# FNet plus PEER layer on one core: adds for the rows of y on GpSimd, an earlier tie for the key scale, half of each token group normalized by VectorE, and the third chunk's weights split eight blocks sooner

## The chip, the cores and the metric

One core of a Trainium2 chip runs the whole kernel. The time is device microseconds of one execution, the median of several. A core has TensorE (PE, matrix products; its weight loads are listed as PEld), VectorE (DVE), ScalarE (ACT), GpSimd (POOL) and SyncE (SP, which issues most of the DMAs here). Each engine works through its own queue in order and waits on semaphores for what others make.

## The reference, cut to what matters

`x` has 2048 tokens of 512 numbers. The result is a sum of three parts, the last two from the layernormed tokens `xn`:

```
xn  = layernorm(x)
# FNet: real part of a DFT over the hidden dimension, then over the sequence
a, b = xn @ dft_hid_re.T, xn @ dft_hid_im.T
y    = dft_seq_re @ a - dft_seq_im @ b
# PEER: 32 heads; two sets of 64 keys of 128 numbers; 4096 experts
q      = xn @ w_q                                # 32 heads x (128 + 128)
s1, s2 = q1 @ k1.T, q2 @ k2.T                    # 64 scores each
take the best 2 of s1 and of s2, of the 4 sums the best 2, g = softmax of these
out    = sum over heads and both: g * gelu(xn . u[expert]) * v[expert]
return x + y + out
```

## The kernel before, in words

The Python text lists instructions; a scheduler of the framework then fixes the order in which each engine gets them, from their dependencies, their place in the text and its own estimate of times. So a text that comes later can still stand earlier in a queue, and several lines of the kernel exist only to tie an instruction to another (a copy with scale 0, a one-element copy into a buffer) so that it is not placed too soon.

**Tokens.** The 2048 tokens are 16 tiles of 128, in four groups of four (`g`, with tiles `q` 0 to 3). Groups are worked in the order `G = (1, 0, 2, 3)`; `n` is a group's place in that order. `ln(g, n)` (L331) makes mean and variance of four tiles, on VectorE (L356 `bn_stats`, L357 the aggregate into `mvs`) or, for two tiles of the second group and one of the fourth, on ScalarE (L342, L343). Then ScalarE takes a square root for the whole group (L360), and VectorE works out `rstd` (L364) and `negm` (L365). `ln_norm(g, n)` (L370) normalizes the four tiles in place, on VectorE (`norm`, L308) or on ScalarE (L379). Group 0, the second in order, uses for its tiles 2 and 3 a masked pair `nm0` in place of `negm` and `rstd`.

**First part of FNet.** `fold` (L402, its first instruction is L409, its last are L412 and L413) adds and subtracts mirrored tokens and columns on VectorE and leaves `Q`; `main` (L433, products at L442) multiplies `Q` with parts of the sequence matrix on TensorE, once per group for the real and once for the imaginary part. `sides` and `evict` finish this, with results in buffers that later hold `u`.

**Scores.** Instead of making `q`, the kernel multiplies `w_q` with the keys first: M = w_q·k, per chunk of four heads, eight chunks (`NCH`). `m_load` (L130) loads a chunk's `w_q` in four parts; `m_mul` (L135) multiplies with the keys (in f32 at L147 for the first two chunks, split in f16 parts at L143 for the others); `m_parts` (L218) writes M as a f16 high part (ScalarE, L221) and a f16 low part (VectorE, L222), four pieces each. The scales come from `w_scale` (L211), seven small VectorE instructions (L589, L118, L119, L121, L214, L215, L216), of which L589 is the tie:

```
nc.vector.tensor_scalar(wsc[:, 0:1], rstd[:, G[1], 0:1], 0.0, 1e-13, op0=ALU.mult, op1=ALU.add)
w_scale(wtot, wsc[:, 0:1])
```

It multiplies a number by 0 and adds 1e-13, the lower limit of the scale, so its only effect is when it can run. For the third and later chunks `m_prep(j, t, ...)` (L150) splits part `t` of the weights of chunk `j` (counted from 0): a f16 copy on ScalarE (L157), a scaled f32 copy on GpSimd for two of the parts (L161) and on ScalarE for the other two (L159), and the subtraction on GpSimd (L162). `s_mm` (L243, products at L247) makes the scores of one token tile for one chunk in 12 products, in the order of the four pieces of M. Eight tiles of the first chunk are done ahead, by `early` (L273), while FNet's first part still runs; `stage` (L509) gives each tile its split form (L514, L515) and its transpose by DMA (L516).

**The loop over chunks and tiles** (from L941) runs over `j` and `i`; block `j * 16 + i` is one token tile of one chunk. `scores` (L878) has ScalarE evict the product (L889) and VectorE find the best (L893, L897). Around it the text hangs other work on block numbers: `HID` names the blocks at which `y_rows` (L687) makes one block of rows of `y`, and ten blocks later `y_store` (L698) writes it with three DMAs on SP; `todo` holds the splits of weights, the filling of `u` and `v` (L772 to L774) and more; `MST` names the tiles after which `m_stage` lets TensorE multiply the next chunk's weights; and the weights of chunk `j + 2` are loaded at tile 9 of chunk `j`. `routing` (L807) turns the best scores of a finished chunk into expert numbers and gates, partly on GpSimd (L822 to L862), with an exponential on ScalarE (L830).

**Rows of y.** `y_rows` calls `hid` (L519): four f32 products on TensorE into one PSUM bank (L521 to L524), seven ScalarE instructions that take the bank apart (L528 to L530), and four adds that combine even and odd columns in place (L533, L534). The bank comes from the two small pools (`pb`, `pc`, two banks each) that `m_mul` uses too.

**After the chunks** come the experts: products with `u` (L1025), gates written out as one-hot products (L1053 to L1063), products with `v` (L1108), the final sums, and tests of the symmetry of the DFT matrices hung in between. The change does not touch them.

Of the kernel before, what the change touches and what calls it, by code (L numbers as in the profile page):

```python
# [15 lines left out]
ALU = mybir.AluOpType  # L16
# [6 lines left out]
NT = S // P  # L23
H = 32
NCH = 8
# [9 lines left out]
def tile_fnet_peer(ctx, tc, x, ca, cb, c5, wt, wf, wr, wq, kt, ut, vn, out):  # L35
# [9 lines left out]
    nc = tc.nc  # L45
# [28 lines left out]
    mvs = cst.tile([P, 4, 4, 2], F32, name="mvs")  # L74
    rstd = cst.tile([P, 4, 4], F32, name="rstd")
# [16 lines left out]
    wsc = cst.tile([P, 4], F32, name="wsc")  # L92
# [87 lines left out]
    def m_fit(j, junk):  # L180
        nc.scalar.activation(junk, M[j][0][:, 0], AF.Abs, accum_out=fits[:, NW + 32 + j:NW + 33 + j])
# [29 lines left out]
    def w_scale(total, low):  # L211

        p, q = pow2(None, MP[0], "pw", 2, total, low)
        nc.vector.tensor_scalar(wsc[:, 0:2], q, 2.0 ** 19, None, op0=ALU.mult)  # L214
        nc.vector.scalar_tensor_tensor(sm0, q[:, 0:1], 2.0 ** 27, q[:, 1:2], op0=ALU.mult, op1=ALU.mult)  # L215
        nc.vector.scalar_tensor_tensor(inv1, p[:, 0:1], 2.0 ** -29 / XS, p[:, 1:2], op0=ALU.mult, op1=ALU.mult)  # L216
# [23 lines left out]
    def xn(g, q):  # L240
        return xp[2 * g + q // 2][:, q % 2]
# [49 lines left out]
    G = (1, 0, 2, 3)  # L291
# [15 lines left out]
    def norm(dst, src, i):  # L307
        nc.vector.tensor_scalar(dst, src, mvs[:, i // 4, i % 4, 0:1], rstd[:, i // 4, i % 4:i % 4 + 1],  # L308
                                op0=ALU.subtract, op1=ALU.mult)
# [60 lines left out]
    def ln_norm(g, n):  # L370
        for q in (0, 2, 1, 3):
            t = xn(g, q)
            b, r = negm[:, g, q:q + 1], rstd[:, g, q:q + 1]
            if g == 0 and q > 1:
                b, r = nm0[:, 0, q - 2:q - 1], nm0[:, 1, q - 2:q - 1]
            if n in (0, 3) and q % 2 == 0:
                norm(t, t, 4 * g + q)
            else:
                nc.scalar.activation(t, t, AF.Identity, bias=b, scale=r)  # L379
# [139 lines left out]
    def hid(t, ims, n, pre, pn, pim, bank):  # L519

        nc.tensor.matmul(bank[:n, 0:129], pre[0], wfs[:, 0:129], start=True, stop=True)  # L521
        nc.tensor.matmul(bank[:n, 129:257], pre[1], wfs[:, 129:257], start=True, stop=True)
        nc.tensor.matmul(bank[:n, 257:384], pim[0], wfs[:, 257:384], start=True, stop=True)
        nc.tensor.matmul(bank[:n, 384:512], pim[1], wfs[:, 384:512], start=True, stop=True)  # L524
        for d, v, a in ((t[:, 2:256:4], bank[:n, 0:127:2], 0), (t[:, 4:256:4], bank[:n, 1:127:2], 1),
                        (t[:, 256:258], bank[:n, 127:129], 1), (t[:, 513:514], bank[:n, 127:128], 1),
                        (t[:, 0:1], bank[:n, 128:129], 1)):
            nc.scalar.activation(d, v, AF.Identity, bias=pn[:, a:a + 1])  # L528
        nc.scalar.activation(t[:, 1:256:2], bank[:n, 129:257], AF.Copy)
        nc.scalar.activation(ims, bank[:n, 257:512], AF.Copy)  # L530
        for a, b, im in ((2, 259, ims[:, 0:127]), (1, 258, ims[:, 127:255])):
            e = slice(a, 256, 2)
            nc.vector.tensor_tensor(t[:, b:513:2], t[:, e], im, op=ALU.add)  # L533
            nc.vector.tensor_tensor(t[:, e], t[:, e], im, op=ALU.subtract)  # L534

    def load_x(g):
        for h in range(2):
# [48 lines left out]
    load_x(G[3])  # L586
    load(0, G[3], behind_stage)
    ln(G[1], 1)
    nc.vector.tensor_scalar(wsc[:, 0:1], rstd[:, G[1], 0:1], 0.0, 1e-13, op0=ALU.mult, op1=ALU.add)  # L589
    w_scale(wtot, wsc[:, 0:1])  # L590
    main(0, G[0])
    for kd in range(KD):
# [10 lines left out]
    for i in TO[4:6]:  # L603
        stage(i)
    ln(G[2], 2)
    ln_norm(G[2], 2)
    for b in range(4, 6):
        early(b)
# [105 lines left out]
    def part_b(safe, stS, stP, stE, xt, u_sb, cmp_p, w4):  # L714
# [10 lines left out]
        def behind(src, at):  # L725

            if at is None:
                return src
            nc.scalar.activation(at, src, AF.Copy)
            return at  # L730
# [4 lines left out]
        def am_load(which, g):  # L735
            nc.sync.dma_start(uf[15].rearrange("p (c f) -> p c f", c=2),
                              uvs[which][2 * g:2 * g + 2].rearrange("c p f -> p c f"))

        def absmax(which, g, at):
            nc.scalar.activation(uf[15], uf[15], AF.Abs, scale=behind(one, at), accum_out=asums[:, g, which:which + 1])  # L740
# [160 lines left out]

        MST = {1: 1, 3: 2, 5: 3, 6: 4, 8: 5, 10: 6} if safe else {3: 1, 4: 2, 5: 3, 7: 4, 8: 5, 9: 6}
        MST0 = MST if safe else {}
        HID = {13: 8, 14: 0, 15: 1, 16: 2, 17: 3, 30: 4, 31: 5, 32: 6, 33: 7}
        todo = [[] for _ in range(NCH * NT)]
        if safe:
            for which in range(2):
                for g in range(16):
                    am_load(which, g)
                    absmax(which, g, None)  # L910
            uv_scale()
            for t in range(7):
                m_stage(0, wq_tile, t)
        else:
            am_load(0, 0)
            for which, n in ((0, 10), (1, 15)):
                todo[n].append(lambda at, w=which: absmax(w, 0, at))
            todo[10].append(lambda at: am_load(1, 0))
            todo[18].append(lambda at: uv_scale())
            todo[20].append(lambda at: m_fit(0, uf[15].bitcast(F16).rearrange("p (k n) -> p k n", k=KD)))  # L920
            todo[(NCH - 1) * NT + 6].append(
                lambda at: m_fit(NCH - 1, MP[0].tile([P, 2, KD, 512], F16, tag="m", name="mj")[:, 0]))
            for j in range(2, NCH):
                for t in range(4):
                    todo[(j - 1) * NT + 2 * t - 4].append(
                        lambda at, j=j, t=t: m_prep(j, t, wqp, behind(sw, at)))
        fills = [(0, g) for g in (0, 1, 2, 3, 8, 9, 10, 11, 12, 13, 14, 4, 5, 6, 7, 15)] + [(1, g) for g in range(V2)]
        slots = [29, 31, 36, 43, 45] + [16 * j + i for j in range(3, 7) for i in (4, 6, 11, 13)]
# [12 lines left out]
        for j in range(NCH):  # L941
            if j + 1 == NCH:
                wq_st.close()
            if j == 0 and not safe:
                vals, idx = EV, EX
            else:
                vals = sp.tile([P, NT, 2, 8, HC], F32, tag="vals", name=f"vals{j}", bufs=2)
                idx = sp.tile([P, NT, 2, 8 if safe else 2, HC], U16, tag="idx", name=f"idx{j}", bufs=2)
            if j == 0 and not safe:
                for a, b in ((0, NT),):  # L950
                    nc.vector.tensor_copy(EV[:, a:b, :, 0, :], M[1][0][:, 1, 3, 8 * a:8 * b].rearrange(
                        "p (i w h) -> p i w h", w=2, h=HC))
            for i in range(NT):
                spare = scores(j, i, vals, idx)
                for t, f in ((j * NT + i, y_rows), (j * NT + i - 10, y_store)):
                    if t in HID and not safe:
                        f(HID[t])
                if j == 1 and not safe:
                    nc.sync.dma_start(xt_d[i], xt[i].rearrange("p a k n -> p (a k n)"))
                mst = MST if j else MST0  # L960
                if j + 1 < NCH and i in mst:
                    m_stage(j + 1, wq_tile, mst[i])
                if j == 0 and i == 6 and not safe:
                    alloc_v(0, V2)
                if j == 0 and 9 <= i < 13 and not safe:
                    sums(i - 9)
                if j + 2 < NCH and i == 9:
                    m_stage(j + 2, wq_tile, 0)
                if i in (1, 2, 4) and pend is not None:
                    routing((0, 2, None, 1)[i - 1], *pend)  # L970
                if j + 1 == NCH and i in (4, 7, 8):
                    routing((4, 7, 8).index(i), j, vals, idx, 0, 4, nc.vector)
                if j + 1 == NCH and i == NT - 1:
                    for b in range(2):
                        compact(b, z[:, b].rearrange("p w k t h -> p (w k t h)"), cmp_p, f"cmp{b}")
                    nc.sync.dma_start(z_d[2:4].rearrange("i p f -> p i f"),
                                      z[:, 2:4].rearrange("p i a k t h -> p i (a k t h)"))
                for n, f in enumerate(todo[j * NT + i]):
                    f(spare[:, n:n + 1])
            pend = (j, vals, idx)  # L980
# [374 lines left out]
        for ph in phases[2:]:  # L1355
            if ph[0] == "z":
                n = 4 * len(ph[1:]) - 2
# [21 lines left out]
        for n, ph in enumerate(phases):  # L1379
            if ph[0] == "z":  # L1380
                b = ph[1:]
# [7 lines left out]
            b = ph[1]  # L1389
# [44 lines left out]
    with tc.If(rv > 0):  # L1434
        with tc.tile_pool(name="gen", bufs=1) as gp, \
# [16 lines left out]
            for i in range(NT):  # L1452
                t = gload(x[i % 4, i // 4], [P, D], "x", f"gx{i}")
                norm(t, t, i)
                gx.append(gsplit(t, [P, D], "xs", f"gxs{i}", 1.0 / XS, NT))
            for q in range(4):
                ya = gp.tile([P, 4, D], F32, tag="ya", name=f"gya{q}")
                for ri in range(2):
                    pp = [gps.tile([P, 512], F32, tag="gp", name=f"gp{q}{ri}{d}", bufs=4)
                          for d in range(KD)]  # L1460
                    for i in range(NT):
                        t = gp.tile([P, 512], F32, tag="c", name=f"gc{q}{ri}{i}", bufs=2)
                        g, sq = divmod(i, 4)
# [14 lines left out]
                    for kd, pieces in enumerate((((0, 1, P, 0), (P - 1, 0, 1, 2)), ((0, 1, P, 1), (P - 1, 0, 1, 0)),  # L1478
                                                 ((0, 0, 1, 1), (1, 1, P, 2)), ((0, 0, P, 3),))):
                        t = gp.tile([P, 512], F32, tag="c", name=f"gw{q}{ri}{kd}", bufs=2)  # L1480
# [3 lines left out]
                    for a in range(4):  # L1484
                        py = pb(f"gy{q}{ri}{a}")
                        n = 0
# [9 lines left out]
                        b = 4 * a + q  # L1496
# [55 lines left out]
```

## Time and profile before

| | |
|---|---|
| time, median of 3 runs | 1153.36 us (1151.84 to 1153.71) |
| the profiled execution's own time | 1150.41 us |
| its span, first to last instruction | 1148.5 us |
| mean granted TensorE clock | 0.996 of full speed |
| busy: TensorE, weight loads, VectorE, ScalarE, GpSimd | 1132.9, 724.5, 945.2, 602.9, 229.0 us |
| scores and FNet | up to 420 us into the span |
| experts | from 420 us to the end |
| DMA, mean over the span | 146 GB/s |

The span's stages are read from the chain of work that ended last, in which TensorE's first product with `u` (L1025) stands at 420.54 us. Busy times overlap; a busy engine can still have nothing to do with the end. The busy time of TensorE counts matmuls whose ends are modelled, so its holes are a better guide than its share.

### The profile page before, as it was taken

What the parts mean: (1) busy time and instruction counts of PE and PEld (TensorE: products, weight loads), DVE (VectorE), ACT (ScalarE), POOL (GpSimd) and SP (SyncE); (2) the same over time, 40 slices, a digit from 0 to 9 for tenths busy, and PEclk for the clock granted to TensorE, in tenths of its full rate; (3) what the DMA queues carried; (4) which work ended last, traced back from release to release, by engine and by line L of the source; (5) the groups of instructions that cost most, each with busy time, mean ns of one, the idle gap of its engine ahead of it and who ended that gap; (6) DMA issues with size and microseconds to landing.
All of it is one profiled execution on the core that took longest, in us unless ns stands there. A gap on an engine that the chain in (4) does not pass through costs nothing.

```text
span 1148.5 us, 25267 instructions
## 1 busy us (share of the span) xinstructions
PE 1132.9 (99%) x9884; PEld 724.5 (63%) x9884; DVE 945.2 (82%) x2851; ACT 602.9 (52%) x1051; POOL 229.0 (20%) x229
## 2 busy tenths in 40 slices
PE   7999999999999999999999999999999999999997
PEld 5465554544545469687488478479569569558763
DVE  7899999899899999956985895896896796888570
ACT  6556687687687644353445445435536436433440
POOL 1303366675774400000000000000010010000000
PEclk8999999999999999999999999999999999999999
DMA  9973345234232105352742742743644555452423
GB/s 293 298 167 153 123 154 202 93 111 163 68 138 72 59 15 142 106 178 79 247 149 88 260 149 93 235 164 105 213 161 147 178 166 169 157 175 66 130 75 104
DMA packets 98334, 167.81 MB, mean 146 GB/s; under 512 B 32916, under 2 KB 48155, under 8 KB 98206
## 3 DMA queue, kind: packets, MB, share of 16 engines
q1 hardware_dynamic: 97904, 166.04, 44.6%
q8 instruction: 79, 1.29, 0.5%
q14 instruction: 49, 0.40, 0.1%
q10 hardware_dynamic: 302, 0.08, 0.0%
HBM read 142.69 MB, written 17.63 MB: 140 GB/s over the span
## 4 chain that ended last, share of the span: by engine, by line
PE 88%; DVE 8%; DMA 2%; ACT 1%; POOL 0%; issue 0%; SPq 0%; POOLq 0%; ACTq 0%
PE z L1025 29%; PE v L1108 28%; PE s L247 23%; PE g L1063 4%; PE p L442 2%; DVE vals L893 1%; PE m L143 1%; DVE idx L897 1%; DVE u L533 1%; DVE u L893 1%; DMA xt_d<-xq 1%; DVE u L897 1%; PE m L147 1%; DMA uv<-in_vn_dram 1%; DVE L L1053 0%; DVE u L534 0%
## 5 line engine op out<-in xcount | busy, mean ns | idle before, releaser
L1025 PE MATMUL z<-xb,u 128*128 128x256 f16 (+1 forms) x3840 | 342.7, 251 | 0.2 <-ACT w L1032 0.2
L1025 PEld LDWEIGHTS <-u 128*128 128x128 f16 x3840 | 309.7, 98 | 26.6 <-issue 0.3
L247 PE MATMUL s<-m,xq 128*128 128x512 f16 x1344 | 298.6, 380 | 4.5 <-DVE m L222 4.5
L1108 PE MATMUL v<-v,act 128*128 128x512 f16 x1056 | 233.2, 379 | 0.0
L247 PEld LDWEIGHTS <-xq 128*128 128x128 f16 x1344 | 130.1, 98 | 156.7 <-issue 7.7
L1053 DVE TENSOR_TENSOR L<-io_lam,cmp 128x2048 f16<-128x2048 f16 x128 | 156.0, 1219 | 59.4 <-PE g L1063 59.4
L1108 PEld LDWEIGHTS <-act 128*128 128x128 f16 x1056 | 101.4, 98 | 117.6
L1121 POOL TENSOR_TENSOR y<-y,xr 128x512 f32<-128x512 f32 x15 | 27.0, 1803 | 610.6 <-DMA y<-y_d 492.0
L1032 ACT ACTIVATE act<-z,scl 128x256 f32<-128x256 f32 (+1 forms) x152 | 72.4, 502 | 120.2 <-PE z L1025 120.2
L893 DVE MAX8 vals<-ss 128x8 f32<-128x64 f32 x896 | 133.9, 216 | 0.0
L1108 PE MATMUL v<-v,w 128*128 128x512 f16 x480 | 106.2, 379 | 0.0
L1184 ACT ACTIVATE cx<-cx 128x896 f32<-128x896 f32 x64 | 60.5, 945 | 70.2 <-DVE cx L1164 49.2
L889 ACT ACTIVATE ss<-s,wsc 128x512 f32<-128x512 f32 x120 | 79.7, 682 | 31.7 <-PE s L247 18.3
L897 DVE FIND_INDEX8 idx<-vals,ss 128x8 uint16<-128x256 f32 x224 | 93.9, 419 | 0.0
L1078 ACT ACTIVATE act<-w 128x1024 f16<-128x1024 f32 x36 | 48.3, 1358 | 60.5 <-DVE w L1071 60.1
L1108 PEld LDWEIGHTS <-w 128*128 128x128 f16 x480 | 46.1, 98 | 53.4
L1071 DVE SCALAR_TENSOR_TENSOR w<-act,scl,g 128x1024 f32<-128x1024 f32 x44 | 55.6, 1274 | 19.8 <-ACT act L1032 19.8
L1158 DVE TENSOR_TENSOR cx<-cx 128x512 f32<-128x512 f32 (+2 forms) x84 | 48.4, 609 | 24.4 <-DMA cx<-in_cb_dram 23.1
L1063 PEld LDWEIGHTS <-L 128*128 128x128 f16 x2048 | 60.6, 96 | 11.2 <-DVE R L1061 1.3
L1079 DVE TENSOR_TENSOR act<-w,act 128x1024 f16<-128x1024 f32 x44 | 60.3, 1372 | 3.7 <-ACT act L1078 3.7
L1061 DVE TENSOR_TENSOR R<-R,cmp 128x512 f16<-128x512 f16 x128 | 61.5, 481 | 1.5
L1063 PE MATMUL g<-R,L 128*128 128x32 f16 x2048 | 61.7, 176 | 0.3 <-DVE R L1061 0.2
(317 smaller groups left out, 1316.6 us busy)
## 6 DMA issues: line engine op xcount, KB each, us to landing
v<-v_d SPq DMA_DIRECT2D x67, 512.0 KB
cx<-in_cb_dram SPq DMA_DIRECT2D x64, 448.0 KB
w<-in_wq_dram SPq DMA_DIRECT2D x28, 512.0 KB
fit<-in_wq_dram SPq DMA_DIRECT2D x28, 512.0 KB
uv<-in_vn_dram SPq DMA_DIRECT2D x16, 512.0 KB
uv<-in_ut_dram SPq DMA_DIRECT2D x16, 512.0 KB
c<-in_ca_dram SPq DMA_DIRECT2D x8, 512.0 KB
y<-y_d SPq DMA_DIRECT2D x16, 256.0 KB
```

What stands on the lines that cost most here:

```text
L247: nc.tensor.matmul(ps, xt[i][:, l, kd, :], m[:, r, kd, :], start=(n == 0), stop=(n == 3 * KD - 1))
L889: nc.scalar.activation(s, ps, AF.Copy, scale=inv)
L893: nc.vector.max(vals[:, i, w, :, h], s[:, g, :])
L897: nc.vector.max_index(idx[:, i, w].rearrange("p k h -> p (k h)"), vals[:, i, w, 0:2].rearrange("p k h -> p (k h)"), s[:, w * HC:g + 1, :]. ...
L1025: nc.tensor.matmul(ps if n == 1 else ps.rearrange("p (b n) -> p b n", b=2), ug[:, l, c % 2, kd, :], xb2[:, k0, r, kd, :] if n == 1 else xb ...
L1032: nc.scalar.activation(ACT[bb][:, cg * m:cg * m + m, :], pv[:, i], AF.Gelu_apprx_tanh, scale=zsc)
L1053: nc.vector.tensor_tensor(L.rearrange("p t (l two) -> p t l two", two=2), io_lam.rearrange("p (l two) -> p l two", two=2).unsqueeze(1).to_ ...
L1061: nc.vector.tensor_tensor(Rv, Rv, bc(2, NC), op=ALU.mult)
L1063: nc.tensor.matmul(p[:, hf, t * NC:(t + 1) * NC], L[:, t, :], R[:, t, :], start=True, stop=True)
L1079: nc.vector.tensor_tensor(w16[..., 1], w, w16[..., 0], op=ALU.subtract)
L1108: nc.tensor.matmul(pv, w16[:, c, :, l], v_sb[g][:, r, cc, :], start=(n + cc == 0 and k == 0), stop=(n == 15 and cc == 1 and k == 2))
L1184: later.append(lambda: nc.scalar.activation(tf[:, P:], tf[:, P:], AF.Abs, accum_out=chk[:, n:n + 1]))
```

## The change

Five places, all before the experts:

- The four adds of each block of rows of `y` in `hid` go from VectorE to GpSimd.
- The tie of the key scale reads the mean of the second group's tile 3 (`mvs`) in place of that group's `rstd`.
- `ln_norm` normalizes tiles 0 and 2 on VectorE in every group; before, only in the first and the fourth. Tile 2 of group 0 takes its masked pair on VectorE in the form multiply, then add.
- Blocks 4 to 7 of the rows of `y` come at blocks 29 to 32, before at 30 to 33.
- The third chunk's weights (`j` = 2) are split at blocks 4, 6, 8 and 10, before at 12, 14, 16 and 18; and their loads are listed at tile 0 of the first chunk, before at tile 9. Other chunks keep their places.

```
@@ ln_norm
-            if n in (0, 3) and q % 2 == 0:
+            if q % 2 == 0 and g == 0 and q > 1:
+                nc.vector.tensor_scalar(t, t, r, b, op0=ALU.mult, op1=ALU.add)
+            elif q % 2 == 0:
                 norm(t, t, 4 * g + q)
             else:
                 nc.scalar.activation(t, t, AF.Identity, bias=b, scale=r)
@@ hid
-            nc.vector.tensor_tensor(t[:, b:513:2], t[:, e], im, op=ALU.add)
-            nc.vector.tensor_tensor(t[:, e], t[:, e], im, op=ALU.subtract)
+            nc.gpsimd.tensor_tensor(t[:, b:513:2], t[:, e], im, op=ALU.add)
+            nc.gpsimd.tensor_tensor(t[:, e], t[:, e], im, op=ALU.subtract)
@@ tie of the key scale
-    nc.vector.tensor_scalar(wsc[:, 0:1], rstd[:, G[1], 0:1], 0.0, 1e-13, op0=ALU.mult, op1=ALU.add)
+    nc.vector.tensor_scalar(wsc[:, 0:1], mvs[:, G[1], 3, 0:1], 0.0, 1e-13, op0=ALU.mult, op1=ALU.add)
@@ part_b
-        HID = {13: 8, 14: 0, 15: 1, 16: 2, 17: 3, 30: 4, 31: 5, 32: 6, 33: 7}
+        HID = {13: 8, 14: 0, 15: 1, 16: 2, 17: 3, 29: 4, 30: 5, 31: 6, 32: 7}
@@
-                    todo[(j - 1) * NT + 2 * t - 4].append(
+                    todo[(j - 1) * NT + 2 * t - (12 if j == 2 else 4)].append(
                         lambda at, j=j, t=t: m_prep(j, t, wqp, behind(sw, at)))
@@
-                if j + 2 < NCH and i == 9:
+                if j + 2 < NCH and i == (9 if j or safe else 0):
                     m_stage(j + 2, wq_tile, 0)
```

(`safe` marks a second copy of this code, with other scales, which is not entered for these inputs.)

## The prediction

> **What bounds the kernel now.** I read the page first, then busy time by stretches, then the order of instructions in the stretches where TensorE stood still. Span and TensorE's busy time come from the page:
>
> ```profile
> span 1148.5 us, 25267 instructions
> PE 1132.9 (99%) x9884; PEld 724.5 (63%) x9884; DVE 945.2 (82%) x2851; ACT 602.9 (52%) x1051; POOL 229.0 (20%) x229
> ```
>
> TensorE is idle for 1148.5 - 1132.9 = 15.6 us. The table by stretches says where (start:end, length, then busy time of PE, PEld, DVE, ACT, POOL, and the granted clock):
>
> ```profile
> 21.34:22.40 1.06, 0.01 (x1) 0.00 (x0) 1.06 (x5) 1.06 (x3) 0.00 (x0) 1.00 1.01 190
> 22.40:25.86 3.46, 0.00 (x1) 0.00 (x0) 2.74 (x10) 3.46 (x7) 0.00 (x0) 0.50 0.95 205
> 25.86:29.20 3.34, 3.34 (x8) 1.13 (x8) 3.34 (x8) 2.12 (x6) 0.00 (x0) 0.50 1.00 397
> ...
> 25.86:80.07 54.21, 54.21 (x220) 28.01 (x220) 48.43 (x107) 30.63 (x60) 11.06 (x19) 0.97 0.84 238
> 80.07:168.62 88.55, 86.89 (x552) 47.59 (x552) 86.62 (x460) 60.33 (x142) 38.75 (x38) 1.00 0.46 152
> 168.62:1130.00 961.38, 960.90 (x8936) 628.76 (x8936) 791.02 (x2227) 495.07 (x818) 175.23 (x152) 1.00 0.42 138
> ```
>
> One hole of 4.5 us ends at 25.86, one of 88.55 - 86.89 = 1.66 us ends at 168.62, and half a microsecond is spread over the next 961 us; the rest lies ahead of the first hole and after the last matmuls, where the change touches nothing. VectorE is busy 86.62 of 88.55 us in the stretch to 168.62, but TensorE hardly notices, so relief for VectorE is worth only what it takes out of the two holes. Their rows in order of time (start, length, engine, line, in brackets the idle time before and its releaser):
>
> ```profile
> 25.86 12.16 PE L247 MATMUL s<-m,xq 128*128 128x512 f16 x48 [4.51 <-DVE m L222]
> ...
> 168.62 0.22 PE L143 MATMUL m<-sums,wh 128*128 128x64 f16 x2 [1.66 <-ACT u L530]
> ```
>
> The first hole has a second price. The granted clock falls to 0.50 about 1.06 us after TensorE falls idle and stays there to 29.20: 8 matmuls take 3.34 us. The other 40 of the 48 take 12.16 - 3.34 = 8.8 us, 0.22 each, so the eight lose 3.34 - 8 x 0.22 = 1.6 us. The most that the change can give at these places is 4.5 + 1.6 + 1.66 = 7.8 us. By the Trainium skill ("TensorE: Matmul & The Clock Gate", Part 1: The HAM clock gate) the clock halves only after an idle window of about 3.4 us; here it fell sooner, so a shortened hole could still cost the 1.6 us, and a rival below counts that.
>
> **The key scale.** The first hole is the wait for the first chunk's M = w_q·k, which ScalarE (L221) and VectorE (L222) write as two halves once the scale is known:
>
> ```profile
> 16.52 0.17 DVE L357 BATCH_NORM_AGGREGATE mvs<-sums 128x2 f32<-128x6 f32 x1
> ...
> 17.67 3.68 PE L147 MATMUL m<-k_sb,wq 128*128 128x64 f32 x32
> ...
> 20.96 0.81 ACT L379 ACTIVATE x<-x,negm,rstd 128x512 f32<-128x512 f32 x1 [1.97 <-DVE negm L365]
> ...
> 21.10 0.14 DVE L589 TENSOR_SCALAR wsc<-rstd 128x1 f32<-128x1 f32 x1
> ...
> 22.95 0.16 DVE L215 SCALAR_TENSOR_TENSOR wsc<-pw 128x1 f32<-128x1 f32 x1
> ...
> 23.79 2.39 ACT L221 ACTIVATE m<-m,wsc 128x512 f16<-128x512 f32 x4
> ...
> 25.06 2.72 DVE L222 SCALAR_TENSOR_TENSOR m<-m,wsc,m 128x512 f16<-128x512 f32 x4
> ```
>
> The scale's small steps run from L589 at 21.10 to L215, done at 23.11: 2.0 us, with other work between. L589 reads rstd, the end of the group's statistics; after the change it reads the fourth tile's mean, which the aggregate at 16.52 writes by 16.69. So the scale can be known at 16.7 + 2.0 = 18.7. Then L221 (2.39 / 4 = 0.6 each) goes into ScalarE's 1.97 idle microseconds from 18.99 on. TensorE finishes w_q·k piece after piece, 3.68 / 4 = 0.9 apart, the last at 21.35; the first three copies can be done by 21.0, the fourth at 22.0, or at 22.8 behind one normalize. VectorE's subtract (2.72 / 4 = 0.68) then ends between 22.7 and, with a statistic in front, 24.2. TensorE starts at 21.35 on the first piece and wants the fourth three quarters into a tile of 12 x 0.22 = 2.6 us, at 23.3. It waits 0 to 0.9 us; I take 0.4, since most of the span is before 23.3. The hole shrinks from 4.5 to 0.4: 4.1 us. With TensorE busy through, the clock does not fall: another 1.6 us (bound below: 0).
>
> **Half of each group on VectorE.** Only the second and third groups change, two tiles each:
>
> ```profile
> L308 DVE TENSOR_SCALAR x<-x,mvs,rstd x2: 540/542/543, 9.0 to 9.4; 128x512 f32<-128x512 f32 x2
> ```
>
> ScalarE loses four normalizes of 0.81 (3.2 us), VectorE gains four of 0.54 (2.2 us). In the second group this gives L221 its room; otherwise the group's fold merely comes sooner. In the third it pays for TensorE's lead: the fold waited for four normalizes, and now waits for two. TensorE's next demands, were it 5.7 us ahead:
>
> ```profile
> 36.60 1.23 DVE L409 TENSOR_TENSOR ft<-x,xq 128x1024 f32<-128x1024 f32 x1 [2.84 <-ACT xq L379]
> ...
> 50.43 0.41 DVE L413 TENSOR_TENSOR q<-fo 128x257 f32<-128x257 f32 x1
> ...
> 55.09 3.60 PE L442 MATMUL p<-c,q 128*128 128x512 f32 x8
> ```
>
> The last group's fold is done at 50.84, TensorE uses it at 55.09: 4.25 us of slack, 1.5 short of 5.7. The fold at 36.60 had idled 2.84 us and loses 2 x 0.8 = 1.6 of it, and the earlier M work takes some 2 us off VectorE's queue ahead of it. So it just holds. I charge 0.3 us.
>
> **The third chunk's split and loads.** Here a cover would be lost without the move:
>
> ```profile
> 83.30 0.62 SPq L133 DMA_DIRECT2D w<-in_wq_dram  x1
> ...
> 102.68 2.85 POOL L161 TENSOR_SCALAR w<-w,wsc 128x1024 f32<-128x1024 f32 x1 [50.67 <-ACT wh L157]
> ...
> 126.86 2.13 POOL L162 TENSOR_TENSOR w<-w,wh 128x1024 f16<-128x1024 f32 x1
> ...
> 130.93 0.22 PE L143 MATMUL m<-sums,wh 128*128 128x64 f16 x2
> ```
>
> GpSimd's last part of that split ends at 128.99, TensorE uses it at 130.93: 1.9 us of slack, so a TensorE 5.7 us ahead would wait 3.8 us. Eight blocks sooner, ScalarE's and GpSimd's parts (2 x 2.85 + 4 x 2.13 = 14.2 us) go where GpSimd had idled 50 us. The loads move from block 9 to block 0, but SP's queue issued the last at 83.30 already, when its buffer came free: nothing, either way. Behind the split's first copy, which can now wait for a load, ScalarE's evictions of scores are queued, but TensorE has four banks to run on. I count 0, up to 1 us of loss.
>
> **The rows of y.** The adds, the second hole, and GpSimd:
>
> ```profile
> L533 DVE TENSOR_TENSOR u<-u 128x127 f32<-128x127 f32 (+3 forms) x18 | 12.0, 669 | 0.0
> L534 DVE TENSOR_TENSOR u<-u 128x127 f32<-128x127 f32 (+3 forms) x18 | 8.7, 488 | 0.0
> ...
> L842 POOL TENSOR_TENSOR if<-if,hoff 128x256 f32<-128x256 f32 x2 | 1.2, 614 | 1.2 <-DVE if L839 1.2
> L847 POOL TENSOR_TENSOR di<-if 128x128 f32<-128x128 f32 x2 | 0.9, 455 | 0.2
> ...
> L533 DVE TENSOR_TENSOR u<-u x18: 272/294/2223, 108.0 to 173.3; 128x127 f32<-128x127 f32 x8, 128x128 f32<-128x128 f32 x8, 1x127 f32<-1x127 f32 x1, 1x128 f32<-1x128 f32 x1
> ```
>
> ```profile
> 157.09 4.34 DVE L533 TENSOR_TENSOR u<-u 128x127 f32<-128x127 f32 x2
> ...
> 159.09 2.19 POOL L774 TENSOR_TENSOR u<-uv,u 128x1024 f16<-128x1024 f32 x1
> ...
> 165.04 0.32 POOL L827 TENSOR_TENSOR c<-c,c 128x64 f32<-128x64 f32 x1 [0.77 <-DVE c L826]
> ...
> 165.39 0.26 ACT L830 ACTIVATE c<-c 128x64 f32<-128x64 f32 x1 [2.59 <-POOL c L827]
> ...
> 168.15 0.42 ACT L530 ACTIVATE u<-hy 128x255 f32<-128x255 f32 x1
> ```
>
> VectorE gets rid of 12.0 + 8.7 = 20.7 us, much of it spent standing behind GpSimd (the median of L533 is 0.294, its mean 0.669): the two adds at 157.09 last 4.34 us, until GpSimd's L774 ends at 161.28. Off TensorE's path this is worth nothing by itself. But the routing's L826 came late for it, so GpSimd's L827 and ScalarE's exp L830, behind which the last row block's evictions stood until 168.57; that bank is TensorE's 1.66 us. The row blocks 4 to 7 now come one tile, 2.6 us, sooner and VectorE is free: the 1.66 us go (bounds 0 and 1.66). Block 8 and blocks 0 to 3 keep their places and add 7.3 us to GpSimd where the moved split has left it free.
>
> With the blocks move their stores, three DMAs each on SP's queue, ten blocks behind. SP stands still for the adds, and the fourth chunk's loads stand behind the stores:
>
> ```profile
> SPq L706 <- DVE u L533: 38.3, 7, 18.8
> ...
> 136.19 0.39 SPq L133 DMA_DIRECT2D w<-in_wq_dram  x1
> ```
>
> An idle GpSimd adds sooner than a full VectorE, so these loads do not come later: nothing, unless the third rival holds. GpSimd gets 16 adds for these four blocks, at 0.455 (same shape) to 0.614 (twice as long): 7.3 to 9.8 us; I take 7.3. The Trainium skill ("GPSIMD Engine Reference", 4.1 Engine selection) puts such two-input work on VectorE, GpSimd being about twice as slow; an estimate by that, twice the 0.294, is 16 x 0.59 = 9.4 us, 2.1 us more of GpSimd's time, which would tell only in the third rival. The rows here have 0.455 against 0.294, a factor of 1.5.
>
> **Sum.** 4.1 + 1.6 + 1.66 - 0.3 = 7.1 us, less 0.4 for GpSimd's queue (next part): 6.7 us. The profiled execution took 1150.41 us, so it becomes 1143.7; that execution lies 2.95 below the median of the runs, 1153.36, so I forecast 1153.36 - 6.7 = 1146.7 for the median.
>
> **Rivals.** *The lead is capped* (0.22): the clock halves all the same (4.1 + 1.66 - 0.7 = 5.1 us), or the last group's fold stays at 50.84 and TensorE's lead ends at 4.25 (4.25 + 1.66 - 0.7 = 5.2). Both give 1148.2. For it: the early fall of the clock, and VectorE's 2.2 us more. Against: the 2.84 us of idle time that the third group gives up.
>
> *The scale stays late* (0.16): its steps keep their place in VectorE's queue behind the statistics, so reading another column changes nothing. The first hole stays, the second goes: 1153.36 - 1.66 = 1151.7. Against: VectorE already takes statistics of the next group in between, so its queue follows readiness.
>
> *GpSimd becomes late* (0.12), the slower side:
>
> ```profile
> 146.94:175.71 28.77, 27.11 (x204) 15.72 (x203) 27.73 (x125) 25.89 (x58) 23.36 (x24) 1.00 0.36 122
> ...
> 173.53 2.18 POOL L162 TENSOR_TENSOR w<-w,wh 128x1024 f16<-128x1024 f32 x1
> 180.55 0.22 PE L143 MATMUL m<-sums,wh 128*128 128x64 f16 x2
> ```
>
> The adds bring a new wait into GpSimd's queue, for ScalarE's L530, and the fourth chunk's split stands behind it. Its last part ends at 175.71, TensorE needs it at 180.55. If GpSimd starts this stretch no sooner than now and fills none of its 28.77 - 23.36 = 5.4 idle us, 7.3 to 9.8 us push that end to 183.0 to 185.5, and TensorE, whatever its lead, is 2.5 to 5.0 us later than before: 1157.1 in the middle. It decides when the split slips by more than 4.84 us. Against: the idle 5.4 us, and that ScalarE, which starts the split, gets its buffers sooner from a freed VectorE; hence the 0.4 us above only.
>
> **Numbers.** The forecast has 0.50, its own range 1145.6 (all 7.8 us) to 1147.8. Runs of this kernel spread over 1.9 us (1151.84 to 1153.71), so about 0.2%, 2.3 us, is what can be told from no change: faster means below 1151.05. The forecast and the capped lead are faster (0.72), the late scale is same (0.16), GpSimd slower (0.12). The range, 1144.7 to 1152.5, leaves out the slow rival and the edge of the late scale.
>
> **What would show it.** Right: VectorE's L589 before 18 us, TensorE's first score matmul before 23 with the clock at 1.00, its first main product of the last group near 49, GpSimd's split of the third chunk done by 105, no idle time ahead of the fourth chunk's products. Wrong: a hole still ending near 25, idle time ahead of L442 behind L413, or ahead of L143 behind GpSimd's L162.

## The result, and the profile after

| | before | after |
|---|---|---|
| time, median of 6 runs each (before's include the three of the forecast's base) | 1152.60 us (1151.18 to 1153.82) | 1147.51 us (1145.46 to 1149.08) |
| ratio | | 0.9961, 95% interval 0.9951 to 0.9971 |
| the profiled execution's own time | 1150.41 us | 1147.81 us |
| busy: VectorE, GpSimd | 945.2, 229.0 us | 929.8, 247.2 us |

By the medians the change saves 5.1 us, by the ratio 4.5 (3.3 to 5.6); 6.7 were forecast. The time itself came out only 0.8 us above the forecast's 1146.7, since the median of before is 0.76 lower here than the base of the forecast. The two profiled executions differ by 2.6 us only, and the first thing to read is why. The order of TensorE's work after the change (line numbers from about 375 on are two higher than before):

```profile
0.98 7.28 PE L550 MATMUL warm<-ones 128*128 128x256 f16 x50 [0.98 <-POOL ones L81]
9.70 4.01 PE L147 MATMUL m<-k_sb,wq 128*128 128x64 f32 x24 [1.43 <-DMA wq<-in_wq_dram]
...
23.89 10.52 PE L247 MATMUL s<-m,xq 128*128 128x512 f16 x48
34.25 3.60 PE L444 MATMUL p<-c,q 128*128 128x512 f32 x8
...
43.87 3.67 PE L444 MATMUL p<-c,q 128*128 128x512 f32 x8 [0.85 <-issue]
...
52.56 3.60 PE L444 MATMUL p<-c,q 128*128 128x512 f32 x8
...
117.35 0.22 PE L143 MATMUL m<-sums,wh 128*128 128x64 f16 x2 [1.07 <-ACT uvpFalse L117]
...
171.55 0.22 PE L143 MATMUL m<-sums,wh 128*128 128x64 f16 x2
171.98 0.20 PE L143 MATMUL m<-sums,w 128*128 128x64 f16 x1 [0.21 <-POOL w L162]
```

The hole of 4.51 us is gone: the 48 score products at 23.89 follow the products with the keys without a wait and take 10.52 us instead of 12.16. The hole of 1.66 us is gone too. There are three new ones: 0.85 ahead of the third group's main product (43.87), 1.07 ahead of the third chunk's products (117.35) and 0.21 in those of the fourth (171.98). The stretches with their clock:

```profile
12.00:18.00 6.00, 6.00 (x22) 4.83 (x22) 4.51 (x11) 3.72 (x12) 1.55 (x5) 0.50 1.01 398
25.86:29.20 3.34, 3.34 (x17) 1.54 (x16) 2.98 (x6) 2.39 (x7) 0.00 (x0) 1.00 0.98 373
80.00:170.00 90.00, 88.93 (x587) 48.95 (x586) 74.97 (x437) 61.25 (x142) 55.32 (x80) 1.00 0.43 153
```

The clock is now 1.00 from 25.86 to 29.20, where it was 0.50. But it is 0.50 from 12 to 18, which the profiled execution of before did not have. That is no work of the change. The 50 warm-up matmuls ahead of everything end at 8.26 here and the first weights land at 9.70; in before's profiled execution the idle time there was 0.59 us, and the clock stayed up. Of the 62 runs of the kernel before that stood beside the first eight experiments, 31 had a mean granted clock of 0.993 and average 1152.46 us; 27 had 0.994 or 0.996 and average 1150.91 (two had 0.992 and two 0.995). The profiled executions have 0.996 without the dip (before) and 0.993 with it (the second experiment). If the mean clock tells the starts of the other runs apart, about one start in two loses 1.5 us by the dip; that reading is argued, since those runs have no trace. The profiled execution from which the forecast was worked out, 2.95 us under the median, was one without. A fair pair of traces has the same start. The second experiment below leaves both holes of before in place and its profiled execution has the dip; beside it the change reads so (the last column is against the second experiment):

| TensorE reaches (us) | before, no dip | second experiment, dip | after, dip | after is ahead by |
|---|---|---|---|---|
| first score product | 25.86 | 27.56 | 23.89 | 3.67 |
| second group's main product | 37.86 | 39.95 | 34.25 | 5.70 |
| third group's main product | 46.47 | 48.56 | 43.87 | 4.69 |
| last group's main product | 55.09 | 57.17 | 52.56 | 4.61 |
| last part of the fourth chunk's products | 180.55 | 182.63 | 177.81 | 4.82 |

The lead of 5.7 us that the prediction works with (4.1 + 1.6) is there at the second group, as 3.67 us of waiting and 2.03 of clock. The fifth experiment, which has the dip and changes nothing in the first 60 us, reaches the second group's main product at 39.62; against it the lead is 5.4. One microsecond of it is lost at the third group's fold; then 1.07 and 0.21 are lost and the 1.66 us gained.

What VectorE does around the scale, M's low parts (L222), the next groups' statistics (L356) and the third group's fold, ScalarE at 117, and GpSimd's splits and adds (the last two lines by groups):

```profile
19.91 0.14 DVE L591 TENSOR_SCALAR wsc<-mvs 128x1 f32<-128x1 f32 x1
...
20.94 0.15 DVE L215 SCALAR_TENSOR_TENSOR wsc<-pw 128x1 f32<-128x1 f32 x1
...
22.57 2.98 DVE L222 SCALAR_TENSOR_TENSOR m<-m,wsc,m 128x512 f16<-128x512 f32 x4
...
30.00 0.66 DVE L356 BATCH_NORM_STATS2 sums<-x 128x6 f32<-128x512 f32 x1
...
34.77 0.69 DVE L356 BATCH_NORM_STATS2 sums<-xq 128x6 f32<-128x512 f32 x1
...
42.21 1.22 DVE L411 TENSOR_TENSOR ft<-xq,xq 128x1024 f32<-128x1024 f32 x1
43.35 0.42 DVE L414 TENSOR_TENSOR q<-fo 128x257 f32<-128x257 f32 x1
43.68 0.42 DVE L415 TENSOR_TENSOR q<-fo 128x257 f32<-128x257 f32 x1
```

```profile
115.11 1.28 ACT L832 ACT_TABLE_LOAD   x1
116.40 0.26 ACT L832 ACTIVATE c<-c 128x64 f32<-128x64 f32 x1
116.56 0.67 ACT L891 ACTIVATE ss<-s,wsc 128x512 f32<-128x512 f32 x1
117.13 0.16 ACT L117 ACTIVATE uvpFalse<-uvs 128x2 f32<-128x2 f32 x1
```

```profile
88.27 6.31 POOL L162 TENSOR_TENSOR w<-w,wh 128x1024 f16<-128x1024 f32 x3
```

```profile
L535 POOL TENSOR_TENSOR u<-u 128x127 f32<-128x127 f32 (+3 forms) x18 | 8.0, 468 | 9.6 <-ACT u L532 9.6
L536 POOL TENSOR_TENSOR u<-u 128x127 f32<-128x127 f32 (+3 forms) x18 | 8.0, 466 | 0.0
```

L591, the tie, runs at 19.91. The third group's last two steps (L414, L415) end at 43.77 and 44.10; right ahead of them stands L411 of the last group, 1.22 us. The profile names no releaser for TensorE's 0.85 us, but the wait ends 0.10 us after L414. And ScalarE's copy L117, which frees the bank of `uv_scale`, stands behind the exponential's table load (1.28 us), the exponential and an eviction.

### The profile page after: what moved, and what is told of

Read it like the earlier page. It is cut to its first block, busy times and chain, and to the rows that moved or that the text cites. A ratio compares the mean times of both kernels' runs of the same rounds, so it can differ in the third digit from the quotient of the medians.

```text
span 1146.0 us, 25270 instructions
## 1 busy us (share of the span) xinstructions
PE 1134.4 (99%) x9884; PEld 726.5 (63%) x9884; DVE 929.8 (81%) x2819; ACT 600.7 (52%) x1047; POOL 247.2 (22%) x265
## 4 chain that ended last, share of the span: by engine, by line
PE 78%; DVE 12%; POOL 4%; DMA 2%; ACT 1%; issue 1%; SPq 0%; DVEq 0%; POOLq 0%; ACTq 0%
PE v L1110 28%; PE z L1027 27%; PE s L247 16%; PE g L1065 4%; DVE vals L895 3%; DVE idx L899 2%; PE m L143 1%; PE m L147 1%; DVE u L895 1%; POOL w L161 1%; DVE L L1055 1%; PE p L444 1%; DVE u L899 1%; DMA u<-in_vn_dram 1%; DVE act L1081 1%
```

## The experiments

Each is told by what it takes from the change; "the hunk" is that of the diff above.

**1. The tie alone.**

```
-    nc.vector.tensor_scalar(wsc[:, 0:1], rstd[:, G[1], 0:1], ...
+    nc.vector.tensor_scalar(wsc[:, 0:1], mvs[:, G[1], 3, 0:1], ...
```

> The kernel before with the tie of the key scale reading the mean of tile 3, and nothing else of the change. Theory (the scale is the cause, ScalarE's normalizes are second): L589 runs before 19 us and the scale is known by 21; the idle time that ends at the first score product falls from 4.5 to between 0.4 and 2.5 us, and the clock stays at 1.00 if that is under about 1 us. Time 1148 to 1150, against 1152.6 of the kernel before. Rival (the four normalizes on ScalarE are the cause): the first copy L221 still stands behind them, the idle time stays over 3 us, time 1151 to 1152.5.

1147.96 us, 0.9967 (0.9957 to 0.9977). One line of the five edits brings nearly the whole gain. The first hole is gone entirely, though ScalarE still has all four normalizes: L221 now stands ahead of them. The tie itself runs at 19.57, not before 19 as expected. TensorE waits at the last group instead:

```profile
52.96 3.67 PE L442 MATMUL p<-c,q 128*128 128x512 f32 x8 [1.01 <-issue]
```

Later it waits 0.62 us at 117.38 for L117, here without a table load ahead of it and with the third chunk's split in its old place, and 0.83 us at 166.52 ahead of the fourth chunk's products.

**2. The halves alone** (the hunk of `ln_norm`).

> The kernel before with tiles 0 and 2 of the second and third groups normalized by VectorE, and nothing else of the change. Theory: the scale still ends near 23 us, so the idle time before the first score product stays between 3 and 4.5 us and the clock halves as before; time 1151.5 to 1152.6. Rival (normalizes are the cause): the idle time falls under 2.5 us, time under 1150.

1152.19 us, 1.0001 (0.9992 to 1.0010): nothing. The scale is late, so the hole stays (3.60 us behind a dip, where experiment 5, with the old normalizes, has 3.18):

```profile
27.56 12.55 PE L247 MATMUL s<-m,xq 128*128 128x512 f16 x48 [3.60 <-DVE m L222]
```

**3. Tie and halves together** (both hunks).

> Tie and halves together, without the adds on GpSimd, the sooner row blocks and the sooner split. Theory: the idle time of 4.5 us and the half clock behind it (1.6 us) go as in the whole change, and the third group's fold takes back 0.9; TensorE is 4 to 5 us ahead at 80 us. The third chunk's split keeps its place, so TensorE waits for GpSimd's L162 ahead of the third chunk's products for what the lead is above 1.9 us, 2 to 3 us; the idle time of 1.66 us ahead of the fourth chunk's products may stay too. Time 1149 to 1150.5. Rival (the sooner split covers nothing): no such wait, time 1147 to 1148, and the rest of the change is worth nothing or less.

1147.02 us, 0.9962 (0.9949 to 0.9974), the same as the whole change. Half of the expectation failed: there is no wait for the third chunk's split. GpSimd's last part (`POOL`) and its use (`PE`):

```profile
123.76 2.13 POOL L162 TENSOR_TENSOR w<-w,wh 128x1024 f16<-128x1024 f32 x1
```

```profile
128.65 0.22 PE L143 MATMUL m<-sums,wh 128*128 128x64 f16 x2
```

It ends at 125.89, 2.8 us before it is needed; in before the slack was 1.9. The split is hung on score blocks, so it comes sooner along with TensorE. The rival holds. Ahead of the fourth chunk's products 0.83 us of waiting are left (165.51), half of the 1.66 in before.

**4. The rest without tie and halves** (hunks of `hid` and `part_b`).

> Adds on GpSimd, row blocks one tile sooner and the third chunk's split eight blocks sooner, without tie and halves. Theory: the first idle time stays at 4.5 us with its half clock, that of 1.66 us ahead of the fourth chunk's products goes, and about 1 us comes ahead of the third chunk's products, where the bank of the scale of u and v is late; time 1151.5 to 1152.5. Rival (the row blocks are worth their 1.66 us, and the wait for the bank comes only with TensorE's lead): time 1150.5 to 1151.2, no idle time ahead of the third chunk's products. Rival (GpSimd late): time over 1154, idle time behind L162.

1150.43 us, 0.9988 (0.9979 to 0.9997). The hole ahead of the fourth chunk is 0.18 us and there is none at the third. The first rival holds: the rest is worth about 1.4 us by itself. Beside tie and halves it adds nothing that can be told (0.9961 for the whole change, 0.9962 for experiment 3).

**5. The adds alone.**

```
-            nc.vector.tensor_tensor(t[:, b:513:2], t[:, e], im, op=ALU.add)
+            nc.gpsimd.tensor_tensor(t[:, b:513:2], t[:, e], im, op=ALU.add)
```

(and the subtraction likewise)

> The kernel before with the four adds of each row block on GpSimd, and nothing else of the change. Theory (the adds held VectorE, and with it the routing and the exponential in front of the evictions): the idle time of 1.66 us ahead of the fourth chunk's products falls under 0.5 us. The third chunk's split keeps its place, where the adds now stand in GpSimd's queue: its last part ends up to 4 us later than at 128.99, which is 0 to 2 us of idle time ahead of the third chunk's products. Time 1150.5 to 1153. Rival (the one tile by which the blocks come sooner removes the idle time, not the adds): 1.66 us stay, time 1151.8 or more.

1155.03 us, 1.0028 (1.0019 to 1.0038): slower. The hole that the adds were to remove has grown:

```profile
133.52 0.20 PE L143 MATMUL m<-sums,w 128*128 128x64 f16 x1 [0.61 <-POOL w L162]
...
172.58 0.27 PE L143 MATMUL m<-sums,wh 128*128 128x64 f16 x2 [3.08 <-ACT u L530]
```

```profile
165.21 0.87 POOL L533 TENSOR_TENSOR u<-u 128x127 f32<-128x127 f32 x2
166.04 0.88 POOL L534 TENSOR_TENSOR u<-u 128x127 f32<-128x127 f32 x2
...
169.01 0.32 POOL L827 TENSOR_TENSOR c<-c,c 128x64 f32<-128x64 f32 x1 [0.16 <-DVE c L826]
```

```profile
169.36 0.26 ACT L830 ACTIVATE c<-c 128x64 f32<-128x64 f32 x1 [4.26 <-POOL c L827]
...
171.13 0.96 ACT L528 ACTIVATE u<-hy,ps 128x64 f32<-128x64 f32 x5
...
172.11 0.42 ACT L530 ACTIVATE u<-hy 128x255 f32<-128x255 f32 x1
```

The routing on GpSimd, up to L827 at 169.01, now stands behind the adds; the exponential waits 4.26 us for it, and the last row block's evictions, still behind the exponential, end at 172.53. The hole goes from 1.66 to 3.08 us. The third chunk's split is late as well, by 0.61. Neither the theory nor the rival foresaw a longer hole. The profiled execution, 1157.39 us, is the slowest of the ten; behind the 3.08 us its granted clock falls to 0.50, from 171.6 to 178.4, so the wait costs more than its own length.

**6. Row blocks 4 to 7 one tile sooner, alone.**

```
-        HID = {..., 30: 4, 31: 5, 32: 6, 33: 7}
+        HID = {..., 29: 4, 30: 5, 31: 6, 32: 7}
```

> The kernel before with row blocks 4 to 7 one tile sooner, and nothing else of the change. Theory (the adds on VectorE are the cause of the late exponential): the idle time ahead of the fourth chunk's products stays above 1 us, time 1151.5 to 1152.5. Rival (the tile is the cause: ScalarE's evictions of the last row block then stand ahead of the exponential): the idle time is gone, time 1150.1 to 1150.8.

1150.91 us, 0.9992 (0.9983 to 1.0001). No hole from 80 to 180 us; the evictions now stand ahead of the exponential:

```profile
162.34 1.09 ACT L528 ACTIVATE u<-hy,ps 128x64 f32<-128x64 f32 x5
...
163.32 0.55 ACT L530 ACTIVATE u<-hy 128x255 f32<-128x255 f32 x1
...
166.32 0.26 ACT L830 ACTIVATE c<-c 128x64 f32<-128x64 f32 x1 [1.41 <-POOL c L827]
```

The rival holds by the trace; the time agrees with it, though its interval just reaches 1.

**7. The clock alone.**

```
+    for i in range(32):
+        nc.tensor.matmul(PP[0][0][0][:, 0:256], zz, w16, start=False, stop=False)   # zz: zeros
     m_parts(0, MS[0, "p"])
```

> The kernel before with 32 matmuls of zeros on TensorE (128 x 256, f16, weights zero, added to a bank of the first main products, so that the output stays the same) put into the idle time before the first score product, to hold the clock up without making anything sooner. Theory (the half clock behind the idle time costs 1.6 us by itself): they fill 3.4 us from the end of the products with the keys, the first score product starts where it did, near 26, the granted clock is 1.00 behind it, the 48 score products take 10.5 instead of 12.2 us, time 1150.2 to 1150.8. Rival (the next fold or bank would have held TensorE anyway): the 48 products are faster, but idle time appears later, and time is within 0.5 us of the kernel before.

```profile
23.52 3.66 PE L595 MATMUL p<-ones,zz 128*128 128x256 f16 x32
27.02 10.52 PE L247 MATMUL s<-m,xq 128*128 128x512 f16 x48
37.38 3.60 PE L442 MATMUL p<-c,q 128*128 128x512 f32 x8
```

The mechanism is shown: with TensorE kept busy, 48 score products take 10.52 us at a clock of 1.00, against 12.55 in the second experiment, whose profiled execution has the same dip at the start, and the second group's main product comes at 37.38 instead of 39.95 (0.54 us of that is the sooner first score product). The time is 1151.34 us, 0.9997 (0.9988 to 1.0005): between a gain of 1.4 us and a loss of 0.6, so how much of the 1.6 us reaches the end is not resolved. In this profile TensorE later waits 1.5 us near 1044 and 1082 for ScalarE, which stands behind a load of `v`; such waits come in some profiles of other kernels here too (0.45 in experiment 6, with another 0.50 behind VectorE) and not in others, and I did not settle what sets them.

**8. The whole change but for the split and its loads** (all but the last two hunks of `part_b`).

> The whole change but for the third chunk's split and loads, which keep their old blocks. Theory of the prediction (GpSimd's split keeps its time while TensorE comes sooner): TensorE waits 1 to 4 us for L162 ahead of the third chunk's last products, time 1148.5 to 1151. Rival (the split's start is paced by the score blocks, so it comes sooner by the lead that TensorE has, and the move covers nothing; the kernel with tie and halves alone had no such wait): no idle time there over 0.5 us, and the wait of 1.07 us for the bank of the scale of u and v, which the earlier split may have made, is smaller too; time 1146.5 to 1147.5.

1151.47 us, 0.9998 (0.9989 to 1.0007): without this edit the gain is gone.

```profile
130.14 0.20 PE L143 MATMUL m<-sums,w 128*128 128x64 f16 x1 [1.01 <-POOL w L162]
...
174.85 0.20 PE L143 MATMUL m<-sums,w 128*128 128x64 f16 x1 [2.48 <-POOL w L162]
```

```profile
127.97 2.12 POOL L162 TENSOR_TENSOR w<-w,wh 128x1024 f16<-128x1024 f32 x1
...
172.67 2.12 POOL L162 TENSOR_TENSOR w<-w,wh 128x1024 f16<-128x1024 f32 x1
```

GpSimd's L162 is late twice, by 1.01 and 2.48 us. Behind the second wait the granted clock is 0.50 from 175.9 to 179.3: from 174.85 to the last part of the fourth chunk's products, at 182.37, TensorE takes 7.52 us, where before took 5.88 (174.67 to 180.55), another 1.64 us. The three together, 5.1 us, use up the lead: experiment 2, without tie, has that last part at 182.63. The expected wait came, at the low end of 1 to 4 us, but not for the expected reason. The lead without the adds makes no wait for the third chunk's split (experiment 3), the adds without the lead 0.61 us (experiment 5), both 1.01: the move covers mainly the adds, which stand in front of the split on GpSimd.

**9. Tie, halves and the sooner row blocks; no adds on GpSimd, no sooner split.**

> Tie, halves and row blocks 4 to 7 one tile sooner; the adds stay on VectorE, the third chunk's split keeps its place. Theory (the tie makes the gain, the sooner tile removes the wait ahead of the fourth chunk's products, the adds on GpSimd cost what the sooner split pays back): the idle time of 0.84 us near 43.8 stays, those of 0.83 near 165 and of 1.07 near 117 are under 0.4 us; time 1145.7 to 1147. Rival (adds and split are needed once TensorE is ahead): idle time over 1 us between 80 and 180, time 1147.5 or more.

1145.17 us, 0.9947 (0.9935 to 0.9958), under the expected 1145.7. Its profiled execution has no dip at the start and shows the other form of it:

```profile
0.98 8.30 PE L550 MATMUL warm<-ones 128*128 128x256 f16 x50 [0.98 <-POOL ones L81]
...
22.01 10.52 PE L247 MATMUL s<-m,xq 128*128 128x512 f16 x48 [0.32 <-DVE m L222]
...
42.33 3.67 PE L444 MATMUL p<-c,q 128*128 128x512 f32 x8 [1.18 <-issue]
...
51.01 3.60 PE L444 MATMUL p<-c,q 128*128 128x512 f32 x8
```

Against before without dip, TensorE is 37.86 - 32.37 = 5.5 us ahead at the second group's main product, and 55.09 - 51.01 = 4.1 at the last. From 80 to 180 us there is no hole at all.

**10. The same, with the second group left to ScalarE.**

```
-            if n in (0, 3) and q % 2 == 0:
+            if n != 1 and q % 2 == 0:
```

> As before this, but in the second group all four tiles are normalized by ScalarE again (two each stay with VectorE in the first, third and fourth group). Theory (VectorE's queue up to the third and the last fold is what caps TensorE's lead, and the second group's fold has slack): second main product still without a wait, third group's without the 0.84 us, the last group's fold 0.5 to 1.1 us sooner; TensorE reaches the last group's main product near 51.7 instead of 52.5; time 0.3 to 0.9 us under the kernel with the halves of all groups. Rival (ScalarE becomes the later one, as with the tie alone, where the last main product waited 1.01 us): idle time of 0.5 us or more ahead of the third or last main product, time the same or up to 0.5 us more.

1144.75 us, 0.9936 (0.9924 to 0.9948). The third main product waits no more:

```profile
44.52 3.60 PE L442 MATMUL p<-c,q 128*128 128x512 f32 x8
...
53.30 3.67 PE L442 MATMUL p<-c,q 128*128 128x512 f32 x8
```

This execution's dip lasts to 21.3, as that of experiment 12; beside that one (45.49 and 54.17) TensorE is 0.97 and 0.87 us sooner. As expected from VectorE's queue; that the time is lower than in 9 is not resolved (the intervals overlap).

**11. The same, with the scale of u and v at block 17 in place of 18.**

```
-            todo[18].append(lambda at: uv_scale())
+            todo[17].append(lambda at: uv_scale())
```

> The same with the scale of u and v listed one block sooner (block 17 instead of 18). Theory (its PSUM bank is freed late because ScalarE's copy L117 stands behind the exponential's table load): the small idle time ahead of the third chunk's first products goes, 0.3 to 0.6 us less than without. Rival (the copy waits for something else): no difference.

1144.67 us, 0.9941 (0.9926 to 0.9956): no difference from 10, which has no such wait to lose. It leaves the cause open; experiment 12 tests it.

**12. The whole change with that line.**

> The whole change, with the scale of u and v listed one block sooner (block 17 instead of 18). Theory (the bank that the third chunk's products wait for is held by ScalarE's copy L117, which stands behind the exponential's table load and two other instructions): L117 runs near 114, the idle time of 1.07 us at 117.35 is gone; time 0.8 to 1.1 us under the whole change, 1146.4 to 1146.8. Rival (the next bank or GpSimd's split holds TensorE then): idle time of the same size within the next 10 us or ahead of the fourth chunk's products, time as the whole change.

1146.70 us, 0.9953 (0.9940 to 0.9965).

```profile
45.49 3.67 PE L444 MATMUL p<-c,q 128*128 128x512 f32 x8 [0.85 <-issue]
...
172.37 0.20 PE L143 MATMUL m<-sums,w 128*128 128x64 f16 x1 [0.20 <-POOL w L162]
```

```profile
116.43 0.34 ACT L117 ACTIVATE uvpFalse<-uvs 128x2 f32<-128x2 f32 x1
116.79 1.28 ACT L832 ACT_TABLE_LOAD   x1
```

L117 runs ahead of the table load, and the hole of 1.07 us is gone; L117 came at 116.43 in an execution that is 1.6 us later than after's, not near 114. The 0.8 us by which the median is lower fits, but lies inside the intervals.

Experiment 10 beats both kernels: by its ratio 7.4 us against before and 2.9 against the whole change (the intervals, 0.9924 to 0.9948 and 0.9951 to 0.9971, do not meet). Experiments 9 and 11 lie beside it, with intervals that overlap both.

## Why the prediction was right, and where its steps were not

**The key scale: right, and nearly all of the gain.** The hole shrank from 4.5 us to nothing (0.32 where the start has no dip; I took 0.4). The sign "before 18 us" failed: L591 ran at 19.91 (18.73 without the dip), not 16.7. The mean that it reads was written by 18.21 (17.03), and VectorE took the four subtractions of `stage` (L517) first. The scale was still known at 21.1 (19.9), while TensorE's last product with the keys ended at 24.05 (21.69). "First score matmul before 23" held without the dip (22.01), not with it (23.89); "last group's main product near 49" failed in both (51.01 and 52.56).

**The clock: right in place, its size not fixed.** 12.16 to 10.52 us is 1.64 against 1.6; but where the first hole is left, the 48 products take 12.55 us in experiment 2 and 12.79 to 12.87 in experiments 4 to 6, so the price runs from 1.6 to 2.35. The lead of 5.7 came out to the digit partly by luck: beside experiment 2 the wait gave 3.67 where I had 4.1, the clock 2.03 where I had 1.6. Experiment 7 shows the price by itself at that place, but not in the time. In a sentence apart: the Trainium skill ("TensorE: Matmul & The Clock Gate", Part 1) has a free-running window of 3.4 us, which fits that the dips seen here lasted 3.4, 6.8 or 10.3 us.

**Half of each group: this term failed.** I charged 0.3 us, for the last group's fold, and argued that the third group's gives up idle time. In after it is the third that stops TensorE, 0.85 us (1.18 without the dip), and the lead falls from 5.7 to 4.6, from 5.5 to 4.1 without the dip: 1.1 to 1.4 us where I had 0.3. I took VectorE's queue of before, which filled its wait for the scale with the next groups' statistics; with the wait gone all but one of these come after M's low parts, and from 22.6 to 43 VectorE has no gap over 0.35 us. Four normalizes were not room but load. In the second group they brought nothing (experiments 1 and 10). So the rival of the capped lead was half right: the cap exists, at 4.1 to 4.6 us, by another fold; its other branch, the clock, did not come, nor did the rival of the late scale. Its saving, 5.1 to 5.2 us, is nearer to the measured 5.1 than my 6.7, and its time, 1148.2, is 0.7 us off where mine is 0.8: the result does not choose between the two, the traces do. Of my signs of being wrong, two showed in small: idle time ahead of a main product behind the fold's last steps (0.85 us), and 0.21 us ahead of L143 behind L162.

**The split's cover: the edit was needed, for another reason.** I let the lead make a wait of 3.8 us, with GpSimd's times fixed. They are not fixed (experiment 3). The cover that mattered was for the adds (experiment 8). "Done by 105" was right (88.27 + 6.31 = 94.6). ScalarE's second and third copy for that split did wait 2.43 and 0.59 us for their loads, and TensorE shows no hole there, as counted.

**The rows of y: the 1.66 us went, for half of the reason I gave.** The tile did it (6), not the freed VectorE; the adds alone made it 3.08 (5). I had followed VectorE's delay to the exponential, but not put GpSimd's own queue, adds ahead of the routing, in its place. The price of an add was right: 0.468 us in the mean over 18 against 0.455. VectorE, busy 86.62 of 88.55 us before, is now busy 74.97 of 90, and that by itself was worth nothing, as said.

**GpSimd's queue.** I took 0.4; it is 0.21 in the whole change. As a mechanism the third rival is real, 3.5 us of waiting and 1.6 of clock in experiment 8, and what kept it away is the sooner split. The rival had priced the wait alone.

**Not foreseen:** the 1.07 us at 117.35. With the split gone from there, the exponential of the first routing comes ahead of L117. That is not the only way to this wait, since the tie alone has 0.62 us of it without the exponential. The missed terms come to 1.3 to 1.6 us: 0.8 to 1.1 more at the fold and 1.07 at the bank, less the 0.4 that the first hole and the 0.2 that GpSimd's queue did not cost. By the medians 1.6 us lie between forecast and result, by the ratio 2.2, of which the rest stays open.

## What to carry to other kernels

When a wait on an engine goes away, the work that had filled it does not go with it: redraw that engine's queue from the wait on, before counting its later idle time as slack. An operation that is moved to another engine must be placed in that engine's order, in front of what it now delays; here that turned a relief into 2.9 us of loss, which a second edit had to buy back. And take a bundle apart: here one line held nearly the whole gain, and two of the five edits, as far as these runs can tell, only paid for each other.

## What the runs showed of the hardware

How long TensorE stands idle does not by itself say whether its clock falls. In after it fell to 0.50 behind an idle time of 1.43 us (at 11.2, when TensorE had been busy again for 1.5 us), in experiment 8 behind 0.85 and 0.21 (at 12.0). In before it stayed up behind 0.59, and behind the 1.66 ahead of the fourth chunk's products; in experiment 1 behind 1.01, at 52.

When it falls is more regular. In experiment 5 the clock falls at 11.14, 24.80 and 171.57 us, 13.66 and 146.77 apart, which is 4 and 43 times 3.413; in experiment 8 at 12.04 and 175.88, 48 times 3.413 apart. Once down it stayed for 3.4 us (175.9 to 179.3 in experiment 8), 6.8 (22.40 to 29.20 in before, 11.2 to 18.0 in after) or 10.3 (11.0 to 21.3 in experiment 10), multiples of the same 3.4. So the clock changes on a grid of 3.4 us, and how soon it falls after TensorE falls idle depends on where in the grid that happens: 1.06 us in before, about 2.4 in experiments 4 and 6. On before's grid the 1.66 us lie within one step (165.8 to 169.2) and did not bring the clock down, while 1.06 us within another did (19.0 to 22.4). What else decides stays open.

The dip at the start differs from execution to execution of much the same work: the same 50 warm-up matmuls took 7.15 to 8.54 us. In the four profiled executions without the dip the idle time before the first weights was 0.59 us or none, in the ten with it 0.85 or more. Some 1.5 of the 3.6 us over which the kernel before spreads (1150.17 to 1153.73 in the first four experiments) come from there, if the mean granted clock of each run tells the two starts apart.
